# A third buffer for v, a fifth for the exponentials, and stores of x that enter the queue one tile later

## The chip, the core and the metric

The kernel runs on one NeuronCore of a Trainium2 chip. The metric is device time in microseconds (us) of one launch, lower is better. The core has five engines that run side by side, each in its own order and tied to the others by semaphores: TensorE (PE in the rows; PEld is its weight load), VectorE (DVE), ScalarE (ACT), GpSimd (POOL) and SyncE (SP, which here does nothing but issue DMAs). What an engine or a queue has to wait for holds back everything that stands behind it in that engine's order.

## What is computed

Bucketed attention over 4 batches x 8 heads, 768 positions, head dimension 64, and then a mixture of experts on its output.

```python
q_bucket = np.sum(q_bits * powers, axis=-1)          # 6 sign bits of q @ proj; k the same
mask = q_bucket[:, :, :, None] == k_bucket[:, :, None, :]
scores = np.where(mask, scale * np.matmul(q, k.transpose(0, 1, 3, 2)), -1000000000.0)
attn = np.exp(scores - np.max(scores, axis=-1, keepdims=True))
attn = attn / (np.sum(attn, axis=-1, keepdims=True) + 1e-09)
x = np.matmul(attn, v)                                # -> (3072 tokens, 512)
...
e_idx = np.argmax(x @ w_gate + modality_bias[modality_id], axis=1)
out[mask_e] = gate_w[mask_e, None] * (np.maximum(x[mask_e] @ w1[e], 0.0) @ w2[e])
```

## The kernel before

The attention works on 16 pairs of heads, `i` = 0 to 15; pair `i` belongs to batch `i // 4`. While the scores of pair `i` are computed, the operands of pair `i + 2` are prepared and the maxima of pair `i + 1` taken. Each pair has six key tiles `kt`.

- `load(i)` (L110) brings q and k of a pair into `xt`; `load_v(i)` (L116) brings v into `vt`, from a pool of `CFG["v"]` buffers (L100). A new `vt` may be loaded only when TensorE has done the last product with the `vt` that the buffer held, so with two buffers the load for pair `i + 1` waits for the products of pair `i - 1`.
- `turn(i)` (L153) prepares the operands. ScalarE copies `xt` into the rounded `hx` (L166), once for each half x = 0 (q) and x = 1 (k); GpSimd or VectorE subtracts to get the remainder (L168; for the pairs in `RELIEF` both on VectorE); SP issues three SBUF-to-SBUF moves out of `hx` for each half (`move`, L151). `hx` has one buffer: its copy for the next pair waits until all six moves out of it have landed. The moves write into one of three sets of operand tiles, `a_..g` and `b_..g`, and wait until TensorE has finished the scores that used that set.
- `signs(i)` and `patterns(i)` follow, with four more moves out of the b and a tiles.
- `score(i)` (L276) issues score matmuls into two PSUM buffers `pss`; ScalarE takes the exponentials (L285, L292) into a buffer of `pbuf`, `NPB = CFG["npb"]` buffers used in a ring; GpSimd adds each of them to the running sum `sp` (L295). `weigh()` (L306) is the generator that multiplies with v (L319) into `psu`, and ScalarE copies that to `ut` (L324).
- `finish(b)` and `finish_x(b, lo, hi)` (L386) end a batch: per 128-token tile `tt`, four transposes of `ut`, a VectorE multiplication by the reciprocal sums into `xs` (L395, two buffers), and a store of `xs` to `x_d` in DRAM (L397), on SP for batches 0 to 2 and on ScalarE's queue for the last. For batches 0 to 2 the six tiles are spread over two pairs: tiles 0, 1, 2 in the third pair of the next batch and 3, 4, 5 in its fourth (pairs 6 and 7, 10 and 11, 14 and 15).
- `route` scatters a small table entry for each token (L607, six scatters a batch, GpSimd).

The order on TensorE and SP in the attention part is written out by hand: `PLAN` has a string for each `kt`, and each letter advances one generator (S scores, M maxima, T turn of pair `i + 2`, A products with v, L and l the loads, x and y a tile of `finish_x`). ScalarE, VectorE and GpSimd are put in order by the framework's scheduler, from its own model of when inputs are ready. The experts follow (from L713 on), over the SBUF that the attention has given back.

Of the kernel before, what the change touches and what calls it, by code (L numbers as in the profile page):

```python
# [18 lines left out]
B, H, S, D = 4, 8, 768, 64  # L19
# [3 lines left out]
REST = S - MAIN  # L23
NP = B * H // 2
BIG = 2.0 ** 100
CFG = dict(spd=(15,), fxs=3, wy=(0.3, 0.71), hpf=0, he=0, hn=0, hm=0, avp=(1, 2, 3, 4, 5, 6), avs=(2,), early=2, pj=7, w3=(0, 0.9), x3=(0, 1), nmd=1, man=(), man0=2, hpo=0, hpe=0, p0=(0, 1), p1=(0, 0.25), p2=(0, 0.4), p3=(0.4, 0.9), s0=4, rc='DDDD', rq=(1, 2), tq=(3, 3, 1, 1, 0, 0), wh=(0.5, 0.78), ws=(0.78, 1.05), n2=2, psx=2, psm=2, pss=2, npb=4, ut=8, qk=3, v=2, wm=(0, 0.9), wf=(0.04, 1.02), wx=(0.3, 0.71), sub="DPPD", fx='D', fx3='R', raw=4, wp=7, LS=4, LL=7, pn=0, rv=(0,), rs='DDPP', r1=(0, 0.5), r2=(0, 1), avg=1, fub=2, fd=1, pm=(), fj=0, fxe=0.5)
P = 128

LAG = 3
# [53 lines left out]
def attention(ctx, actx, tc, a, x_d, route, setup, early_slots, early_tables, latest, adds, bias):  # L83
    nc = tc.nc
    v = a["v"]
# [3 lines left out]
    spool = ctx.enter_context(tc.tile_pool(name="spool", bufs=2))  # L89
    upool = ctx.enter_context(tc.tile_pool(name="upool", bufs=CFG["ut"]))  # L90
    bp = ctx.enter_context(tc.tile_pool(name="bp", bufs=1))
    bp.tile([P, 48], F32, name="pad2")
    ps_x = ctx.enter_context(tc.tile_pool(name="ps_x", bufs=CFG["psx"], space=PSUM))
    xt = actx.enter_context(tc.tile_pool(name="xt", bufs=2))
    hxp = actx.enter_context(tc.tile_pool(name="hxp", bufs=1))
    gens = []
    for g in range(3):
        opp = actx.enter_context(tc.tile_pool(name=f"opp{g}", bufs=1))
        gens.append({n: [opp.tile([P, 2, S], F32R, name=f"{n}_{h}g{g}") for h in range(2)] for n in ("a", "b")})
    ldv = actx.enter_context(tc.tile_pool(name="ldv", bufs=CFG["v"]))  # L100
    sm = actx.enter_context(tc.tile_pool(name="sm", bufs=4))
    const = actx.enter_context(tc.tile_pool(name="const", bufs=1))
    ps_m = actx.enter_context(tc.tile_pool(name="ps_m", bufs=CFG["psm"], space=PSUM))
    ps_s = actx.enter_context(tc.tile_pool(name="ps_s", bufs=CFG["pss"], space=PSUM))
    flags = actx.enter_context(tc.tile_pool(name="flags", bufs=2))
# [27 lines left out]
    bits = [const.tile([P, HALF], BF16, name=f"bits{j}") for j in range(2)]  # L133
    pbuf = [const.tile([P, 2, S], F32, name=f"pb{j}") for j in range(CFG["npb"])]
    pat32 = pbuf[0][:, 0, 0:512].rearrange("p (a h c) -> p a h c", a=2, h=2)
# [171 lines left out]
    def weigh():  # L307

        for i in range(NPR):
            t = st[i]  # L310
            t["u"] = [ps_u.tile([P, MAIN], F32, name=f"psu{j}") for j in range(2)]
            for part in range(2):
                w = COLS[part].stop - COLS[part].start
                nc.tensor.matmul(t["u"][part][:, 0:w], vsb[i % 2], t["lone"][:, COLS[part]], start=True, stop=False, skip_group_check=True)
            for kt in range(NT):
                for part in range(2):
                    w = COLS[part].stop - COLS[part].start
                    for h in range(2):
                        nc.tensor.matmul(t["u"][part][64 * h:64 * h + 64, 0:w], t["v"][:, h, kt], t["pb"][kt][:, h, COLS[part]], start=False, stop=(kt == NT - 1), skip_group_check=True)  # L319
                if kt == NT - 1:  # L320
                    ut = upool.tile([P, S], F32, name="ut")
                    for part in range(2):
                        w = COLS[part].stop - COLS[part].start
                        nc.scalar.copy(out=ut[:, COLS[part]], in_=t["u"][part][:, 0:w])  # L324
                    t["ut"] = ut
                yield
# [59 lines left out]
    def finish_x(b, lo, hi, pool=bp, n=2, name="xs"):  # L386
        ts_, rin = fin[b]
        xv = x_d[b * S:(b + 1) * S].rearrange("(p t) d -> p t d", t=NT)
        for tt in range(lo, hi):
            xs = pool.tile([P, 512], F32, name=name, bufs=n)  # L390
            xp = ps_x.tile([P, 512], F32, name="psx")
            for c in range(4):
                nc.tensor.transpose(xp[:, c * P:(c + 1) * P], ts_[c]["ut"][:, tt * P:(tt + 1) * P], ident)
            yield
            nc.vector.tensor_tensor(out=xs.rearrange("p (h d) -> p h d", d=D), in0=xp.rearrange("p (h d) -> p h d", d=D),  # L395
                                    in1=rin[:, tt].unsqueeze(2).broadcast_to([P, 8, D]), op=ALU.mult)
            (nc.scalar if b == B - 1 else nc.sync).dma_start(out=xv[:, tt], in_=xs)  # L397
            yield

    def finish_last():  # L400
# [21 lines left out]
    with tc.manual_schedule(engines={mybir.EngineType.PE, mybir.EngineType.SP}):  # L422
# [17 lines left out]
        avs = weigh()  # L440
        fins = xs = ts = iter(())
        for i in range(NPR):
# [6 lines left out]
            for kt in range(NT):  # L449
                for c in (PLAN if i else PLAN0)[kt]:  # L450
# [4 lines left out]
                    elif c == "T":  # L455
                        next(ts, None)
                    elif c == "P":
                        next(last, None)
                    elif c == "A":
                        next(avs)  # L460
                    elif c == "B":
                        if late:
                            late.pop(0)()
                    elif c == "v":
                        vadds(i)
                    elif c == "V":
                        vsums(i)
                    elif c == "Q":
                        if i > 0:
                            sums(i - 1)  # L470
                    elif c == "L":
                        if i + 3 < NPR:
                            load(i + 3)
                    elif c == "l":
                        if 0 < i < NPR - 1:
                            load_v(i + 1)
                    elif c in FIN[i >= NPR - 4][i % 4]:
                        with tc.issue_after(newest[0]):
                            next(fins, None)
                    elif c == "x" and i % 4 == 2 or c == "y" and i % 4 == 3:  # L480
                        if c == "x" and kt == 0 and i > 4:
                            xs = finish_x(i // 4 - 1, 0, NT)
                        next(xs, None)
                        next(xs, None)
        for _ in avs:
            pass
        sums(NPR - 1)
    return finish, finish_x, ps_x, ident


# [518 lines left out]
```

## Time and profile before

| | |
|---|---|
| three runs, us | 799.78, 802.07, 803.81 (median 802.07) |
| profiled execution, us | 803.15, its span 801.4 |
| mean granted TensorE clock | 0.989 |
| busy: PE, PEld, DVE, ACT, POOL, us | 754.0, 522.1, 499.7, 413.5, 438.7 |
| attention part | up to about 490 us, experts from there |

The span runs from the first to the last instruction; the profiled execution's own time lies 1.75 us above it. A busy time is the union of an engine's instructions; weight loads overlap matmuls.

### The profile page before, as it was taken

How to read it: one execution, taken by the hardware profiler on the slowest of the kernel's cores; microseconds unless marked ns; L12 is line 12 of the kernel's file. 1: busy time of each engine (PE TensorE's matmuls, PEld its weight loads, DVE VectorE, ACT ScalarE, POOL GpSimd, SP SyncE). 2: the span in 40 equal slices, each digit the busy share in tenths (PEclk: the TensorE clock that was granted, in tenths of full speed). 3: DMA queues.
4: the chain of work that ended last, by engine and by line, in shares of the span. 5: the costliest groups of instructions: out<-in, count | busy, mean ns of one | idle time of the engine just before them, and what ended most of it. 6: DMA issues, size and time to landing. Idle time of an engine off the chain costs nothing.

```text
span 801.4 us, 11627 instructions
## 1 busy us (share of the span) xinstructions
PE 754.0 (94%) x4060; PEld 522.1 (65%) x4060; DVE 499.7 (62%) x839; ACT 413.5 (52%) x730; POOL 438.7 (55%) x321
## 2 busy tenths in 40 slices
PE   4799999999999899999989999999999999999996
PEld 1555566556565456655555555888888888888885
DVE  6787677578787477787677948764344242752422
ACT  3566676665656466657546456324253334633423
POOL 7298889778869578869847895034120204202002
PEclk9999999999999899999999999999999999999998
DMA  6665534343358333455320275467352435843311
GB/s 204 151 179 158 145 94 136 99 123 107 116 113 155 98 99 107 120 132 159 102 64 25 45 196 201 159 99 229 115 175 81 168 91 178 273 140 124 127 54 60
DMA packets 59573, 104.24 MB, mean 130 GB/s; under 512 B 9709, under 2 KB 30829, under 8 KB 59504
## 3 DMA queue, kind: packets, MB, share of 16 engines
q1 hardware_dynamic: 53424, 88.23, 39.7%
q0 software_dynamic: 4928, 13.14, 5.2%
q10 hardware_dynamic: 1152, 2.03, 0.9%
q8 instruction: 34, 0.56, 0.3%
q14 instruction: 35, 0.29, 0.1%
HBM read 59.89 MB, written 13.33 MB: 91 GB/s over the span
## 4 chain that ended last, share of the span: by engine, by line
PE 65%; DVE 14%; issue 9%; ACT 5%; DMA 4%; POOL 1%; SPq 1%; POOLq 0%; ACTq 0%; DVEq 0%
PE psu L319 12%; PE pss L273 8%; PE pss L274 6%; PE hps L799 4%; PE hps L800 4%; PE hps L801 4%; PE psm L217 4%; PE yps L845 3%; PE yps L843 3%; PE yps L844 3%; PE psm L223 3%; ACT pb L285 2%; DMA x_d<-y 2%; DVE mx L219 2%; PE psx L188 2%
## 5 line engine op out<-in xcount | busy, mean ns | idle before, releaser
L295 POOL TENSOR_TENSOR sp<-sp,pb 128x768 f32<-128x768 f32 x124 | 232.2, 1895 | 18.8 <-ACT pb L292 18.0
L285 ACT ACTIVATE pb<-pss 128x512 f32<-128x512 f32 x192 | 114.1, 598 | 113.8 <-PE pss L274 103.1
L219 DVE TENSOR_REDUCE mx<-psm 128x1 f32<-128x512 f32 x192 | 130.4, 687 | 58.0 <-PE psm L217 57.4
L752 DVE TENSOR_TENSOR w<-raw,w 128x1024 fp32r<-128x1024 f32 x64 | 79.5, 1249 | 96.0 <-ACT w L750 95.4
L319 PE MATMUL psu<-pb,vt 128*64 128x512 f32 (+1 forms) x768 | 134.4, 492 | 0.0
L750 ACT CAST w<-raw 128x1024 fp32r<-128x1024 f32 x64 | 66.9, 1051 | 74.6 <-PE yps L845 65.6
L319 PEld LDWEIGHTS psu<-pb,vt 128*64 128x64 f32 x768 | 50.8, 136 | 69.1 <-issue 58.3
L295 POOL TENSOR_TENSOR sp<-pb,pb 128x768 f32<-128x768 f32 x31 | 58.9, 1920 | 54.1 <-ACT pb L292 54.0
L273 PE MATMUL pss<-a_0g 128*128 128x512 f32 x192 | 80.3, 418 | 7.6 <-ACT pb L285 6.7
L770 POOL DMA_INDIRECT xg<-x_d,tb x18 | 22.8, 1267 | 117.7 <-DMA tb<-tab 112.4
L843 PE MATMUL yps<-w,hl 128*128 128x512 f32 x208 | 82.7, 397 | 0.0
L845 PE MATMUL yps<-w,hh 128*128 128x512 f32 x208 | 81.3, 391 | 0.0
L844 PE MATMUL yps<-w,hh 128*128 128x512 f32 x208 | 81.0, 389 | 0.0
L799 PE MATMUL hps<-xh,w 128*128 128x512 f32 x192 | 75.7, 394 | 0.1
L800 PE MATMUL hps<-xl,w 128*128 128x512 f32 x192 | 74.9, 390 | 0.4 <-DVE xl L789 0.4
L801 PE MATMUL hps<-xh,w 128*128 128x512 f32 x192 | 74.8, 390 | 0.0
L225 DVE TENSOR_REDUCE mx<-psm 128x2 f32<-128x512 f32 x96 | 66.2, 690 | 13.5 <-PE psm L223 11.7
L273 PE MATMUL pss<-a_1g 128*128 128x512 f32 x192 | 69.2, 360 | 3.4 <-ACT pb L292 3.4
L805 ACT ACTIVATE hh<-hps 128x512 fp32r<-128x512 f32 x48 | 28.7, 598 | 73.6 <-PE hps L801 73.6
L274 PE MATMUL pss<-b_0g 128*128 128x512 f32 x192 | 66.1, 344 | 0.0
L274 PE MATMUL pss<-b_1g 128*128 128x512 f32 x192 | 65.7, 342 | 0.0
L806 DVE SCALAR_TENSOR_TENSOR hl<-hps,hh 128x512 fp32r<-128x512 f32 x48 | 33.0, 688 | 50.9 <-ACT hh L805 50.8
(203 smaller groups left out, 1367.4 us busy)
## 6 DMA issues: line engine op xcount, KB each, us to landing
raw<-moe_w SPq DMA_DIRECT2D x64, 512.0 KB, 3.7
xt<-qk SPq DMA_DIRECT2D x31, 384.0 KB, 3.9
vt<-v SPq DMA_DIRECT2D x16, 384.0 KB, 3.9
a_0g<-hx SPq DMA_DIRECT2D x30, 192.0 KB, 3.4
a_1g<-hx SPq DMA_DIRECT2D x30, 192.0 KB, 3.7
x_d<-xs SPq DMA_DIRECT2D x18, 256.0 KB, 2.0
b_1g<-a_1g SPq DMA_DIRECT2D x17, 192.0 KB, 2.9
b_0g<-a_0g SPq DMA_DIRECT2D x17, 192.0 KB, 2.7
```

Source lines behind the costliest of these rows:

```text
L219: newest[:] = [nc.vector.tensor_reduce(out=mx[:, qt + j, 1 - h, 0:1], in_=mp, axis=AX.X, op=ALU.max).ins]
L273: nc.tensor.matmul(out, t["s1"][h][:, ks], t["m1"][h][:, cs], start=True, stop=False)
L274: nc.tensor.matmul(out, t["s2"][h][:, ks], t["m2"][h][:, cs], start=False, stop=True)
L285: nc.scalar.activation(t["pb"][kt][:, h, 0:MAIN], sp, AF.Exp, scale=0.125)
L295: add = (nc.vector if h and i in CFG["spd"] else nc.gpsimd).tensor_tensor(out=t["sp"][:, h], in0=(t["pb"][0] if kt == 1 else t["sp"])[:, h ...
L319: nc.tensor.matmul(t["u"][part][64 * h:64 * h + 64, 0:w], t["v"][:, h, kt], t["pb"][kt][:, h, COLS[part]], start=False, stop=(kt == NT - 1 ...
L799: nc.tensor.matmul(hps, lo[:, c, fs], xh[:, c], start=(c == 0), stop=False)
L800: nc.tensor.matmul(hps, hi[:, c, fs], xl[:, c], start=False, stop=False)
L801: nc.tensor.matmul(hps, hi[:, c, fs], xh[:, c], start=False, stop=(c == 3))
L843: nc.tensor.matmul(yps[g], hl[fc][:, gs], hi[:, fb], start=(fc == 0), stop=False)
L844: nc.tensor.matmul(yps[g], hh[fc][:, gs], lo[:, fb], start=False, stop=False)
L845: nc.tensor.matmul(yps[g], hh[fc][:, gs], hi[:, fb], start=False, stop=(fc == 7))
```

## The change

Two numbers of the table `CFG` are raised: the exponentials get a fifth buffer and v a third. In `finish_x` the store of a tile is no longer issued behind its multiplication: it is kept in the list `done` and issued when the generator is asked for the next tile, ahead of that tile's transposes. The last tile of a batch, and all tiles of the last batch, are stored at once as before.

```diff
 CFG = dict(
...
-    npb=4, ut=8, qk=3, v=2,
+    npb=5, ut=8, qk=3, v=3,
...
+        done = []
         for tt in range(lo, hi):
+            if done:
+                done.pop()()
             xs = pool.tile([P, 512], F32, name=name, bufs=n)
...
             nc.vector.tensor_tensor(out=xs..., in0=xp..., in1=rin..., op=ALU.mult)
-            (nc.scalar if b == B - 1 else nc.sync).dma_start(out=xv[:, tt], in_=xs)
+            done.append(partial((nc.scalar if b == B - 1 else nc.sync).dma_start, out=xv[:, tt], in_=xs))
+            if b == B - 1 or tt == hi - 1:
+                done.pop()()
             yield
```

TensorE and VectorE carry out the same instructions in the same order in both programs. On SP the stores move, on ScalarE some of the `hx` copies, on GpSimd the additions over v (L251 to L253). The names below are tiles; a number behind the last underscore is the tile's buffer or its place in the program. Lines behind the edit are 5 higher in the changed program (a store is L392 when deferred, L402 when issued at once).

SP in pair 7 before, from the moves of half x = 0 for pair 9 to the moves of its signs; `x_d` is the DRAM copy of x, and the three stores are those of tiles 3, 4 and 5 (the number behind `xs` tells them apart):

```order
L151 DMA b_1g2_123<-hx_2380 64x768
L397 DMA x_d_57<-xs_2386 128x512
L397 DMA x_d_57<-xs_2448 128x512
L151 DMA a_0g2_120<-hx_2380 64x768
L151 DMA a_1g2_121<-hx_2380 64x768
L151 DMA b_0g2_122<-hx_2380 64x768
L120 DMA vt_2488<-v 128x2x384
L397 DMA x_d_57<-xs_2490 128x512
L151 DMA b_1g2_123<-b_0g2_122 64x768
```

The same place in the changed program; the numbers of `xs` are one higher for the same tile, so 2252 is tile 2, 2387 tile 3, 2449 tile 4 and 2491 tile 5:

```order
L151 DMA b_1g2_123<-hx_2380 64x768
L392 DMA x_d_57<-xs_2252 128x512
L392 DMA x_d_57<-xs_2387 128x512
L151 DMA a_0g2_120<-hx_2380 64x768
L151 DMA a_1g2_121<-hx_2380 64x768
L151 DMA b_0g2_122<-hx_2380 64x768
L120 DMA vt_2488<-v 128x2x384
L392 DMA x_d_57<-xs_2449 128x512
L402 DMA x_d_57<-xs_2491 128x512
L151 DMA b_1g2_123<-b_0g2_122 64x768
```

The moves of half x = 1 and the load of v stood behind the store of tile 4; they stand behind the store of tile 3 now. At the matching place of pair 6 they stood behind the store of tile 0 and stand behind no store now.

ScalarE in pair 8 before, at the `hx` copies for pair 11 (2973), between the exponentials of key tiles 1 and 2 (`pb1`, `pb2`):

```order
L292 ACTIVATE pb1_161<-pss_2710 128x2x256
L324 COPY ut_2730<-psu0_2537 128x512
L324 COPY ut_2730<-psu1_2538 128x256
L166 CAST hx_2973<-xt_2645 128x768 x2
L285 ACTIVATE pb2_162<-pss_2739 128x512
```

The same place in the changed program, where the ring of five gives these two key tiles the buffers `pb4` and `pb0`:

```order
L292 ACTIVATE pb4_164<-pss_2711 128x2x256
L166 CAST hx_2974<-xt_2646 128x768
L324 COPY ut_2731<-psu0_2538 128x512
L324 COPY ut_2731<-psu1_2539 128x256
L166 CAST hx_2974<-xt_2646 128x768
L285 ACTIVATE pb0_160<-pss_2740 128x512
```

One of the two copies has moved ahead of the copies of `ut`. In pair 7 the copies for pair 10 move further. Behind the copies of `ut` ScalarE runs L285 twice, L292, L285 twice, L292 and `nm` (L235); both copies stood behind that `nm`, and now the first stands behind the first L285 and the second behind the first L292.

## Rows read from the trace of the kernel before

**Rows 1.** The page, busy time of TensorE (share of the span, instructions)

```profile
PE 754.0 (94%) x4060; PEld 522.1 (65%) x4060; DVE 499.7 (62%) x839; ACT 413.5 (52%) x730; POOL 438.7 (55%) x321
```

**Rows 2.** Windows: stretch, length, busy per engine (instructions), clock, DMA share, GB/s

```profile
234.30:270.40 36.10, 31.08 (x162) 17.87 (x166) 21.20 (x35) 19.39 (x37) 29.82 (x22) 0.87 0.75 140
356.50:384.80 28.30, 27.28 (x162) 15.86 (x165) 20.31 (x34) 19.26 (x37) 26.37 (x19) 1.00 0.62 163
```

**Rows 3.** Timeline, TensorE: start, us, instruction [idle before <- what ended it]

```profile
243.34 0.39 PE L273 MATMUL pss<-a_0g 128*128 128x256 f32 x1 [1.82 <-ACT pb L285]
...
265.27 0.58 PE L273 MATMUL pss<-a_0g 128*128 128x256 f32 x1 [3.10 <-ACT pb L285]
```

**Rows 4.** Windows of 4 us behind those two gaps

```profile
244.00:248.00 4.00, 4.00 (x16) 2.77 (x15) 2.06 (x3) 3.68 (x8) 3.82 (x5) 0.57 1.04 123
...
264.00:268.00 4.00, 2.73 (x14) 1.55 (x14) 0.69 (x1) 2.30 (x4) 1.64 (x3) 0.57 0.35 114
268.00:272.00 4.00, 4.00 (x17) 1.40 (x14) 1.63 (x3) 0.60 (x1) 3.77 (x3) 0.57 0.40 98
```

**Rows 5.** Timeline, ScalarE, in pairs 7 and 8

```profile
231.54 1.31 ACT L285 ACTIVATE pb<-pss 128x512 f32<-128x512 f32 x2 [1.46 <-PE pss L274]
...
241.23 1.56 ACT L166 CAST hx<-xt 128x768 fp32r<-128x768 f32 x2 [2.95 <-DMA vt<-v]
...
256.96 0.59 ACT L292 ACTIVATE pb<-pss 128x512 f32<-128x512 f32 x1
259.40 0.86 ACT L324 COPY ut<-psu 128x512 f32<-128x512 f32 x2 [1.85 <-PE psu L319]
263.16 1.56 ACT L166 CAST hx<-xt 128x768 fp32r<-128x768 f32 x2 [2.90 <-DMA vt<-v]
```

**Rows 6.** Timeline, ScalarE, the same copies in pairs 11 and 12

```profile
360.49 1.57 ACT L166 CAST hx<-xt 128x768 fp32r<-128x768 f32 x2
...
379.80 1.57 ACT L166 CAST hx<-xt 128x768 fp32r<-128x768 f32 x2 [0.18 <-ACT ut L324]
```

**Rows 7.** Timeline, SP's issues in pairs 7 and 8

```profile
225.52 6.55 SPq L397 DMA_DIRECT2D x_d<-xs  x2
...
233.32 0.59 SPq L151 DMA_DIRECT2D b_0g<-hx  x1
234.01 0.61 SPq L120 DMA_DIRECT2D vt<-v  x1
...
253.61 0.46 SPq L151 DMA_DIRECT2D b_0g<-hx  x1
259.86 0.39 SPq L120 DMA_DIRECT2D vt<-v  x1
```

**Rows 8.** DMA issues of 232.1 to 234: count, KB each, us to landing

```profile
b_0g<-hx SPq DMA_DIRECT2D x1, 192.0 KB, 7.7
```

**Rows 9.** DMA issues of 247.7 to 254

```profile
b_1g<-hx SPq DMA_DIRECT2D x1, 192.0 KB, 12.9
b_0g<-hx SPq DMA_DIRECT2D x1, 192.0 KB, 9.2
```

**Rows 10.** DMA issues of 366.9 to 371.2

```profile
b_0g<-hx SPq DMA_DIRECT2D x1, 192.0 KB, 4.4
```

**Rows 11.** The page, DMA issues over the whole span, median us to landing

```profile
a_1g<-hx SPq DMA_DIRECT2D x30, 192.0 KB, 3.7
```

**Rows 12.** DMA issues of 232 to 262, then of 354 to 384: the scatters

```profile
tab<-recs,posi POOLq DMA_INDIRECT x6, 7.8
...
tab<-recs,posi POOLq DMA_INDIRECT x6, 5.2
```

**Rows 13.** Waits over the span: us in total, times, longest

```profile
SPq L120 <- PE psu L319: 77.0, 11, 14.6
...
POOL va L251 <- DMA vt<-v: 21.4, 10, 4.3
...
ACT pb L285 <- POOL sp L295: 2.6, 2, 2.3
```

More of the change, by code (lines that the diff above doesn't have):

```diff
@@ L25 @@
 BIG = 2.0 ** 100
-CFG = dict(spd=(15,), fxs=3, wy=(0.3, 0.71), hpf=0, he=0, hn=0, hm=0, avp=(1, 2, 3, 4, 5, 6), avs=(2,), early=2, pj=7, w3=(0, 0.9), x3=(0, 1), nmd=1, man=(), man0=2, hpo=0, hpe=0, p0=(0, 1), p1=(0, 0.25), p2=(0, 0.4), p3=(0.4, 0.9), s0=4, rc='DDDD', rq=(1, 2), tq=(3, 3, 1, 1, 0, 0), wh=(0.5, 0.78), ws=(0.78, 1.05), n2=2, psx=2, psm=2, pss=2, npb=4, ut=8, qk=3, v=2, wm=(0, 0.9), wf=(0.04, 1.02), wx=(0.3, 0.71), sub="DPPD", fx='D', fx3='R', raw=4, wp=7, LS=4, LL=7, pn=0, rv=(0,), rs='DDPP', r1=(0, 0.5), r2=(0, 1), avg=1, fub=2, fd=1, pm=(), fj=0, fxe=0.5)
+CFG = dict(spd=(15,), fxs=3, wy=(0.3, 0.71), hpf=0, he=0, hn=0, hm=0, avp=(1, 2, 3, 4, 5, 6), avs=(2,), early=2, pj=7, w3=(0, 0.9), x3=(0, 1), nmd=1, man=(), man0=2, hpo=0, hpe=0, p0=(0, 1), p1=(0, 0.25), p2=(0, 0.4), p3=(0.4, 0.9), s0=4, rc='DDDD', rq=(1, 2), tq=(3, 3, 1, 1, 0, 0), wh=(0.5, 0.78), ws=(0.78, 1.05), n2=2, psx=2, psm=2, pss=2, npb=5, ut=8, qk=3, v=3, wm=(0, 0.9), wf=(0.04, 1.02), wx=(0.3, 0.71), sub="DPPD", fx='D', fx3='R', raw=4, wp=7, LS=4, LL=7, pn=0, rv=(0,), rs='DDPP', r1=(0, 0.5), r2=(0, 1), avg=1, fub=2, fd=1, pm=(), fj=0, fxe=0.5)
 P = 128
```

## The prediction

> **What bounds the kernel now.** I read the page first, then a table of windows by pair of heads, then the timeline of each engine where two like stretches differ. The reader is to see this. TensorE is busy for 94% of the span, the others for 65% at most [rows 1], so the change can only give what TensorE loses to waits and to a lower clock. Each pair in the attention part takes TensorE some 28 us, from one matmul of the signs to the next. One takes 36.10 us, from 234.3 to 270.4; the pair at the same place of the next batch, 356.5 to 384.8, does the same work with the same letters of the plan and takes 28.30 us, each with 162 records of TensorE [rows 2]. The excess is 36.10 - 28.30 = 7.8 us.
>
> It has two causes, twice each. TensorE stands still for 1.82 us until 243.34 and for 3.10 us until 265.27, both times for an exponential [rows 3]. Behind each stop its clock is granted at a mean of 0.57, between the two levels of 1.2 and 2.4 GHz, in the 4 us from 244 and the 8 us from 264 [rows 4]. Work withheld by the clock is 3 x 0.43 x 4 = 5.2 us, less about 0.6 for the 1.27 us to 265.27 in which TensorE had nothing to run: 4.6. With the idle time, 1.82 + 1.7 = 3.5 us hang on the first stop and 3.10 + 2.9 = 6.0 on the second, 9.5 together. The length of the stretch gives 7.8, since the twin has small gaps of its own; I scale the parts to that: 2.9 and 4.9 us.
>
> What held the exponentials is in ScalarE's order: a copy to hx waited for 2.95 us until 241.23 and another for 2.90 us until 263.16 [rows 5]. The row names the load of v as what ended it, but the copy reads no v: it needs the one buffer of hx free, so all six moves of the pair before landed. Their last was issued at 233.32 and took 7.7 us to land, to 241.0 [rows 7, 8]; in the second case 253.61 + 9.2 = 262.8 [rows 7, 9]. Both fit the copies' starts within 0.4 us. In the twin the same copies begin without such a wait [rows 6].
>
> **The first stop: -2.9 us.** Why was the move as late as 233.32? SP ran into two stores at 225.52 and came out at 232.07 [rows 7]: the second, that of tile 4, waits for VectorE's multiplication, and three moves and the load of v stand behind it. Now the store at that place is tile 3's, which could be issued at 225.52 already, and tile 2's ahead of it waits for nothing new. So the three moves go about 6.5 us earlier, the last at 233.32 - 6.5 = 226.8; at the span's median of 3.7 us [rows 11] it lands at 230.5. ScalarE's first copy has moved up too: it stands behind the first of the two exponentials that begin at 231.54 and take 1.31, so at 232.2 [rows 5]. The margin is 1.7 us and the stop goes. With 7.7 us to land [rows 8] the move lands at 234.5, ScalarE stands for 2.3 us instead of 2.95, and hardly anything is gained: this term lies between -2.9 and -0.3. I take -2.9, because the issue now falls before the stretch of slow landings.
>
> **The second stop: -4.9 us.** The moves for pair 10 wait for TensorE's last scores of pair 7, which come 2.9 us earlier when the first stop goes: the last is issued by 253.61 - 2.9 = 250.7. ScalarE now meets one of the two copies ahead of ut, behind the L292 that ends at 256.96 + 0.59 = 257.55, so at 254.6. If the move takes the twin's 4.4 us [rows 10] it lands at 255.1: half a microsecond late, of which TensorE, with two buffers of scores in front of it, sees nothing. If it takes 9.2 as now [rows 9], it lands at 259.9, ScalarE stands for 5.3 us instead of 2.90, and the stop stays, longer by up to 2.4 us. The term lies between -4.9 and +2.4. Of the two landings 4.4 is nearer to the median of 3.7 [rows 11], and the transfers that were in the queue with these moves, a load of v and three moves, have gone out earlier; I take -4.9.
>
> **The edits that I cost at nothing.** The third buffer of v ends SP's wait for the products, 77.0 us in 11 times, 14.6 at most, and the 21.4 us for which GpSimd waits for v [rows 13]. Behind that load on SP stand four moves whose results TensorE needs for the scores two pairs on, a whole pair (28 us) away; GpSimd follows ScalarE and is busy for 55% [rows 1]. That slack is the cover; were it gone, the longest of the waits, 14.6 us once, would bound the gain, and a load of v that now lands beside moves could cost half a microsecond of landing. The value is 0. The fifth buffer of exponentials ends ScalarE's waits for GpSimd's additions, 2.6 us in two [rows 13]; TensorE's rows name none of them, so -2.6 to 0, value 0. The deferred stores: a tile's multiplication reuses the buffer of two tiles before, whose store now goes out about one tile later. Tile 4's multiplication ends just before 232.07 and needs tile 2's store, issued by 225.52 [rows 7]: over 6 us ahead, value 0, up to the wait of one store if SP is held by moves. The experts keep their instructions and their order on TensorE and VectorE; their buffers lie over those of the attention and shift with them, which I bound by 0.5 us either way, since the additions that read the last exponentials end about where the first hidden layer is written.
>
> **The sum.** 803.15 - 2.9 - 4.9 = 795.35 us for an execution like the profiled one (span 801.4 and 1.75 around it). The median of the runs shown is 802.07, 1.1 lower; I do not know how much of that 1.1 lies in the two stops, so I leave the sum as it is: 795.4.
>
> A rule on the clock gives another sum. The Trainium skill, "TensorE: Matmul & The Clock Gate", section "HAM oscillation", counts a throttled stretch at half of its duration, on top of the idle time that led to it. By that rule the whole 9.5 would be given back and the time would be 793.7; the twin's length says 7.8, and I keep the row.
>
> **Rivals.**
> 1. The second stop stays (27%). Six scatters of the routing table run in each of the two stretches, and their own landings rise and fall with those of the moves: 7.8 us median in the slow one, 5.2 in the twin [rows 12]. The change leaves the scatters alone. If the stretch from 232 to 262 stays slow because of them, only the first term comes: 803.15 - 2.9 = 800.2, and by the median of the runs 799.1. For it: 12.9 and 9.2 us for moves that begin well after the store of tile 4 [rows 9]. Against: the twin has the same six scatters, and its moves take 4.4 [rows 10]. The Trainium skill, "DMA: Bandwidth & Descriptors", section "Specifications", says that transfers below 512 bytes are read, modified and written by the DMA engines; the entries of the table are that small, so the page speaks for this rival, and the difference between the stretches for something besides.
> 2. Slower (11%). ScalarE runs in its written order, and the scheduler has put the hx copies 2 to 6 us further ahead, on its own view of when moves land. The place is pairs 7, 8, 11 and 12; it decides from landings of about 5.4 us on in pairs 7 and 11 (3.7 plus the margin of 1.7). With 7.7 us there and 9.2 in pair 8, ScalarE stands for 2.3, 5.3 and 2.3 us where it now stands for 2.95 and 2.90: 4.0 us more, and one more stretch at the lower clock, 1.7: 803.15 + 5.7 = 808.9.
> 3. No change (15%). The stops are partly this execution's own: the runs spread over 4.0 us, and 799.78 is 3.4 below the profiled execution. If other executions lose little there, or the time comes back as a wait for VectorE behind it, the result is 800 to 803, say 801.5.
>
> **How the numbers follow.** My forecast has 47%, with a range of its own from 792.5 (the sum by the clock's rule, less the 1.1 of the median) to 798. The rivals have 27, 11 and 15%. The range that holds 8 in 10 goes from 791.5, where 2.6 us of the fifth buffer come on top of part of that, to 803.5, which takes in rivals 1 and 3 and leaves out the slower one. Half a percent of 802.07 is 4.0 us, about what a measurement of this kernel can tell from no change: faster is under 798.1, slower over 806.1. Faster holds nearly all of the forecast and a good quarter of rival 1: 54%. Slower is rival 2: 11%. The rest is 35%.
>
> **What would show it.** Right: SP's three moves for half x = 1 of pair 9 issued within a microsecond of the store of tile 3, 6 us ahead of the store of tile 4; no wait in front of the hx copies of pairs 7 and 8; no gap of TensorE over 1 us and no clock under 1 between the signs of pair 9 and of pair 10; that stretch at 28 to 29 us, all others as before. Rival 1 shows a single gap with a lower clock at the copies of `ut` in pair 8. Rival 2 shows waits of ScalarE for DMA in front of hx in pairs 11 and 12, where there are none now. My prediction is wrong if the stretch comes down and the end does not, or if the moves go out early and land as late as before.

## The result

The changed kernel takes 810.31 us (median of 4 runs, 809.66 to 811.06); the kernel before, beside it, 802.83 us (799.78 to 803.81). The ratio is 1.010, interval 1.0074 to 1.0126 (here and below the ratio on record, which is not the quotient of the two medians): the change costs about 7.5 us, where the forecast was a gain of 7.8. The profiled execution of the changed kernel took 810.90 us, with a span of 809.0; the one before took 803.15.

### The profile page after: what moved, and what is told of

Read it like the earlier page. It is cut to its first block, busy times and chain, and to the rows that moved or that the text cites. A ratio compares the mean times of both kernels' runs of the same rounds, so it can differ in the third digit from the quotient of the medians.

```text
span 809.0 us, 11610 instructions
## 1 busy us (share of the span) xinstructions
PE 753.6 (93%) x4060; PEld 522.7 (65%) x4060; DVE 509.0 (63%) x839; ACT 413.3 (51%) x730; POOL 438.4 (54%) x321
## 4 chain that ended last, share of the span: by engine, by line
PE 64%; DVE 13%; issue 10%; ACT 7%; DMA 2%; POOL 2%; SPq 1%; another core or an unknown queue 1%; ACTq 0%; POOLq 0%; DVEq 0%
PE psu L319 11%; PE pss L273 8%; PE pss L274 6%; PE hps L804 4%; PE hps L806 4%; PE hps L805 4%; PE yps L850 4%; PE yps L848 4%; PE psm L217 4%; PE yps L849 4%; ACT pb L285 3%; PE psm L223 2%; DVE b_1g L168 2%; PE psx L188 1%; DVE mx L219 1%
## 5 line engine op out<-in xcount | busy, mean ns | idle before, releaser
L295 POOL TENSOR_TENSOR sp<-sp,pb 128x768 f32<-128x768 f32 x124 | 231.0, 1887 | 46.5 <-ACT pb L292 41.7
L285 ACT ACTIVATE pb<-pss 128x512 f32<-128x512 f32 x192 | 114.1, 598 | 116.2 <-PE pss L274 108.6
L295 POOL TENSOR_TENSOR sp<-pb,pb 128x768 f32<-128x768 f32 x31 | 59.0, 1923 | 40.8 <-ACT pb L292 40.7
L225 DVE TENSOR_REDUCE mx<-psm 128x2 f32<-128x512 f32 x96 | 66.2, 690 | 11.4 <-PE psm L223 9.7
```

The source lines that it names most:

```text
L285: nc.scalar.activation(t["pb"][kt][:, h, 0:MAIN], sp, AF.Exp, scale=0.125)
L295: add = (nc.vector if h and i in CFG["spd"] else nc.gpsimd).tensor_tensor(out=t["sp"][:, h], in0=(t["pb"][0] if kt == 1 else t["sp"])[:, h ...
```

## The profile after

The page, the line that answers [rows 1]:

```profile
PE 753.6 (93%) x4060; PEld 522.7 (65%) x4060; DVE 509.0 (63%) x839; ACT 413.3 (51%) x730; POOL 438.4 (54%) x321
```

No engine has more instructions than before. One has clearly more busy time: VectorE, 509.0 us where it was 499.7. TensorE's is the same, so the span grew by TensorE's waits. The windows of the two stretches of [rows 2], with the same columns, each from the same matmul of the signs to the next:

```profile
234.30:268.90 34.60, 29.35 (x162) 16.82 (x166) 24.13 (x34) 17.98 (x36) 29.31 (x22) 0.90 0.56 123
354.40:388.90 34.50, 29.33 (x163) 17.81 (x166) 24.97 (x34) 17.84 (x35) 27.97 (x21) 0.90 0.57 122
```

The slow stretch has come down only from 36.10 to 34.60, and its twin, 28.30 before, is as slow now. In both VectorE (the third busy time) is busy for 24 to 25 us, against 21.2 and 20.3. Matched record by record (4060 in each), TensorE of the changed kernel stands level with before at 241 us, 3.0 us ahead at 262, 1.7 ahead at 271, 2.0 ahead at 366, 4.1 behind at 386 and 440, and 8.1 behind at 545, from where it stays.

So the first stop is gone. SP's issues, which answer [rows 7]:

```profile
217.82 7.94 SPq L392 DMA_DIRECT2D x_d<-xs  x2
225.86 0.47 SPq L151 DMA_DIRECT2D a_0g<-hx  x1
226.69 0.47 SPq L151 DMA_DIRECT2D a_1g<-hx  x1
227.21 0.59 SPq L151 DMA_DIRECT2D b_0g<-hx  x1
```

The last move of half x = 1 goes out at 227.21, where it was 233.32, and ScalarE's copies to hx in pair 7 wait for nothing, at 231.94 and 233.63 (in [rows 5] the first stood 2.95 us). Then ScalarE in pairs 8 and 12, at the copies of [rows 5, 6]:

```profile
260.97 0.83 ACT L166 CAST hx<-xt 128x768 fp32r<-128x768 f32 x1 [6.44 <-DVE b_1g L168]
...
383.14 0.83 ACT L166 CAST hx<-xt 128x768 fp32r<-128x768 f32 x1 [2.79 <-DVE b_1g L168]
```

It now waits for 6.44 and 2.79 us, and what ends the wait is no transfer: it is VectorE's subtraction L168, which reads the one buffer of hx (at 383.14 one of 1.96 us). TensorE's gaps, which answer [rows 3]:

```profile
263.84 0.58 PE L273 MATMUL pss<-a_0g 128*128 128x256 f32 x1 [4.70 <-ACT pb L285]
...
372.21 0.49 PE L242 MATMUL psx<-identr,nm 128*128 128x128 f32 x2 [3.71 <-ACT nm L235]
...
386.01 0.39 PE L273 MATMUL pss<-a_0g 128*128 128x256 f32 x1 [1.07 <-ACT pb L285]
```

The gap of 3.10 us has become 4.70, and two are new. The clock falls behind the first two, as in [rows 4]; the windows there:

```profile
262.00:266.00 4.00, 2.16 (x10) 1.55 (x14) 1.03 (x2) 2.87 (x6) 0.17 (x1) 0.50 0.66 148
...
374.00:378.00 4.00, 4.00 (x14) 3.42 (x13) 2.33 (x4) 2.45 (x6) 1.65 (x2) 0.50 0.22 53
```

The granted clock there is 0.50, the lower of the two levels. What VectorE does in front of these gaps, timeline of VectorE:

```profile
255.28 5.61 DVE L168 TENSOR_TENSOR b_1g<-xt,hx 128x768 fp32r<-128x768 f32 x1
...
365.24 4.95 DVE L168 TENSOR_TENSOR b_0g<-xt,hx 128x768 fp32r<-128x768 f32 x1
370.11 0.68 DVE L225 TENSOR_REDUCE mx<-psm 128x2 f32<-128x512 f32 x1
```

These are the subtractions L168 of `turn`, which read `hx`. The same instruction on tiles of the same shape takes 0.95 us at 245.12, and 5.61 and 4.95 us here. At 255.28 it holds back the copy to hx and the exponentials behind that; at 365.24 it holds back the maxima of L225, and with them nm, for which TensorE waits. GpSimd beside it:

```profile
254.50 0.98 POOL L612 DMA_INDIRECT tab<-recs,posi  x1 [0.17 <-issue]
255.51 3.61 POOL L295 TENSOR_TENSOR sp<-pb,pb 128x768 f32<-128x768 f32 x2
259.07 0.99 POOL L251 TENSOR_TENSOR va<-vt 128x384 f32<-128x384 f32 x1
...
364.80 0.96 POOL L612 DMA_INDIRECT tab<-recs,posi  x1 [0.30 <-issue]
365.79 3.57 POOL L295 TENSOR_TENSOR sp<-sp,pb 128x768 f32<-128x768 f32 x2
369.53 1.52 POOL L612 DMA_INDIRECT tab<-recs,posi  x1 [0.17 <-issue]
```

Both subtractions begin while a scatter (L612) runs, 0.78 and 0.44 us into it, and end 0.83 us after GpSimd's additions behind it: 259.07 + 0.99 = 260.06 and 260.89, 365.79 + 3.57 = 369.36 and 370.19. The same two places before, GpSimd and then VectorE:

```profile
257.64 4.32 POOL L295 TENSOR_TENSOR sp<-pb,pb 128x768 f32<-128x768 f32 x2 [0.69 <-ACT pb L292]
...
365.84 0.96 POOL L607 DMA_INDIRECT tab<-recs,posi  x1 [0.30 <-issue]
366.82 1.02 POOL L251 TENSOR_TENSOR va<-vt 128x384 f32<-128x384 f32 x1
367.92 1.06 POOL L252 TENSOR_TENSOR va<-va 128x128 f32<-128x128 f32 x1
```

```profile
258.30 1.96 DVE L168 TENSOR_TENSOR b_1g<-xt,hx 128x768 fp32r<-128x768 f32 x1
...
367.29 1.38 DVE L168 TENSOR_TENSOR b_0g<-xt,hx 128x768 fp32r<-128x768 f32 x1
```

In pair 11 the additions over v (L251 to L253) stood behind the fourth scatter. In the changed program they stand behind the first and second, the third and fourth scatters come 1.2 us later in pair 7 and, against TensorE, 1.0 us later in pair 11, and the subtraction meets the long additions L295 instead. In pair 8 GpSimd paused for 0.69 us between the sixth scatter and the additions.

A subtraction that begins in a scatter need not be long. The one of 0.95 us in the changed kernel, and the scatter that it begins in, 0.28 us after its start:

```profile
245.12 0.95 DVE L168 TENSOR_TENSOR b_0g<-xt,hx 128x768 fp32r<-128x768 f32 x1
...
244.84 0.96 POOL L612 DMA_INDIRECT tab<-recs,posi  x1 [0.30 <-issue]
```

Over all traces twelve subtractions out of hx begin in a scatter with GpSimd's work right behind it: the four that begin 0.12 to 0.28 us into it take 0.95 us, the eight that begin 0.43 us or more into it take 4.67 to 5.95.

## The experiments

Three theories were put to the test. A: the loss is VectorE's subtraction behind GpSimd's additions, and it is the third buffer of v that moves GpSimd against VectorE. B: the hx copies, moved ahead in ScalarE's order, do the harm (rival 2 of the prediction). C: a subtraction that begins in a scatter stands behind the additions that follow on GpSimd. Later C was sharpened: additions that follow on a scatter without a break run as a train, and VectorE gets in only where a GpSimd instruction must wait for the one before it. A hand-over is the place where one GpSimd instruction ends and the next begins.

**The parts of the change.** Each is the kernel before with one edit or two.

```diff
 e1_stores_only: the edit of finish_x alone
 e2_v3_only:     -v=2  +v=3
 e3_npb5_only:   -npb=4  +npb=5
 e4_stores_v3:   finish_x and v=3
```

> Stores deferred, v at 2 buffers and the exponentials at 4, as before. On SP, TensorE, VectorE and ScalarE the order is that of the changed kernel; on GpSimd the additions over v move in pairs 7 and 11 only. Theory A (the loss is VectorE's subtraction L168 standing behind GpSimd's additions, and GpSimd's phase comes from the third buffer of v): the first stop goes, the subtractions in pairs 8 and 12 stay near 2 us, the time is 797 to 801. Theory B (the hx copies that were moved ahead on ScalarE cost it, whatever GpSimd does): 806 to 811, with gaps of TensorE over 3 us near 264 and 372 as in the changed kernel.

> Third buffer for v alone. ScalarE, VectorE and TensorE keep the order of the kernel before; GpSimd takes its additions over v earlier in most pairs. Theory A: GpSimd's shifted phase makes one or more of the subtractions L168 of pairs 10 and 14 (in before 1.2 to 2.0 us) take 4 us or more, and the time is 804 to 809. Theory B: the copies stand where they stood, the time is 801 to 804 and both stops of pairs 7 and 8 are there.

> Fifth buffer of exponentials alone; no engine's order changes. Both theories: 801 to 804, no difference from before beyond its spread.

> The change without the fifth buffer of exponentials; every engine's order is that of the changed kernel. Theories A and B: 808 to 812, as the changed kernel. If it is at 803 or below, the fifth buffer is what lets GpSimd come into the way, and both theories miss a part.

| | us | ratio to before (median 801.29), interval | long subtractions, us |
|---|---|---|---|
| stores | 807.30 | 1.0065 (1.0042 to 1.0087) | 4.67 at 255.84, 4.93 at 365.35 |
| v | 801.88 | 0.9995 (0.9972 to 1.0019) | 4.88 at 257.04 |
| exponentials | 801.33 | 0.9995 (0.9972 to 1.0018) | none |
| stores and v | 809.08 | 1.0081 (1.0051 to 1.0110) | 5.62 at 255.29, 4.96 at 365.21 |

The third buffer of v as the cause falls: the deferred stores alone carry most of the loss. With 807.30 us and gaps of TensorE of 3.71 us before 263.41 and 3.69 before 372.31 they came out as theory B expected; only the later runs tell B from C. With v alone one subtraction is long, as theory A expected, and the time is not: TensorE's gap behind it is 3.21 us, about the 3.10 that stood there before. What v adds to the stores (809.08 against 807.30) lies within the intervals, as does what the fifth buffer adds. Every long subtraction began in a scatter with additions right behind it; this is where theory C came from. The first two runs also take the first stop away or shorten it (no gap with stores alone, 1.10 us with v alone).

The profiled execution with the fifth buffer alone (800.53 us) shows something else. ScalarE, VectorE, TensorE and SP have the order of the kernel before, and yet the copies of pair 8 wait for nothing and the second stop is missing:

```profile
262.30 1.57 ACT L166 CAST hx<-xt 128x768 fp32r<-128x768 f32 x2
```

TensorE is 3.6 us ahead by 271 there, while the median, 801.33, is that of the kernel before. So the second stop need not be in every execution.

**The scatters left out.** Both kernels, without the twelve scatters of batches 0 to 2.

```diff
-        for t in range(NT):
+        for t in range(NT if b == B - 1 else 0):
```

> The changed kernel without the scatters of the routing table for batches 0 to 2 (12 of them beside pairs 7, 8, 11 and 12; left out, so the experts gather dummy rows for those tokens). Theory C (a subtraction L168 that begins while GpSimd is in a scatter stands behind all additions that follow without a break): no subtraction takes over 3 us, no gap of TensorE over 1.5 us near 264, 372 and 386, the time is 793 to 798. Theory B (hx copies ahead of ut wait for moves that land late, or for anything else): the gaps stay, 803 to 810.

> The kernel before without the same scatters, as the measure for the run without them of the changed kernel. If the scatters slow the landings of the moves, both stops of pairs 7 and 8 shrink: 795 to 799. If they do not, 800 to 802. Theory C: the changed kernel without scatters is no slower than this one.

The changed kernel takes 799.35 us (0.9970, 0.9946 to 0.9993), 1.4 above what theory C expected; the one before 797.63 (0.9947, 0.9929 to 0.9965), so the changed one is 1.7 us the slower, where theory C expected it to be no slower; the intervals overlap. No subtraction is longer than 2.5 us in either, and at 386 us both stand 6.8 to 7.4 us ahead of the kernel before: without scatters neither has the two stops, so in these traces the stops of before hang on the scatters as well as the new ones (the edit also moves what follows them on GpSimd). The moves out of hx land faster without them: the two b_0g moves of 225 to 262 us take 4.3 us (median), where they took 8.4. The copies to hx are ahead in ScalarE's order in the first of the two and cost little up to there (two gaps of TensorE of 1.04 and 1.05 us that the second run does not have), which speaks against theory B. Its profiled execution (804.93 us, the slowest of its runs) loses 6.6 us near 495; ScalarE waits there for a load of the experts' weights, 3.65 us until 494.75, and TensorE for 4.17 us behind it.

**The additions over v put back.** The changed kernel, with L251 to L253 of pairs 8 and 12 held behind the fourth scatter, as they stood before.

```diff
+        with tc.issue_after(SCATTERED[-3]) if i in (8, 12) else nullcontext():
             nc.gpsimd.tensor_tensor(out=a1, in0=v[:, :, 0:3], ...)
```

> The changed kernel with the additions over v for pairs 8 and 12 put back behind the fourth scatter on GpSimd, where they stood before; SP, ScalarE, VectorE and TensorE as in the changed kernel. Theory C: the subtraction near 365 begins beside the additions over v instead of in a scatter and takes under 2 us; the one near 255 still begins in the sixth scatter and takes over 4: 804 to 807, with the gap near 264 and none near 372. Theory B: no difference from the changed kernel, 809 to 811.

796.96 us, ratio 0.9938 (0.9915 to 0.9962): better than theory C expected, and faster than both kernels, with every copy to hx where the change had put it. That settles B: where the subtractions are short, the copies ahead cost nothing that is seen. No subtraction takes over 2.6 us. The one near 255 us was expected to stay long; it began at 255.75, ahead of the sixth scatter at 256.14, so there it is the moment that changed. GpSimd at the place of pair 11:

```profile
357.66 0.96 POOL L617 DMA_INDIRECT tab<-recs,posi  x1 [0.30 <-issue]
358.64 1.02 POOL L255 TENSOR_TENSOR va<-vt 128x384 f32<-128x384 f32 x1
359.74 1.06 POOL L256 TENSOR_TENSOR va<-va 128x128 f32<-128x128 f32 x1
```

**A second scatter put forward.** The same, with the sixth scatter directly behind the fifth.

```diff
+            if t < NT - 1 and latest:
+                behind = latest[0]
-            with tc.issue_after(latest[0]) if b < B - 1 else nullcontext():
+            with tc.issue_after(behind) if b < B - 1 else nullcontext():
```

> As the run before, and the sixth scatter of a batch put directly behind the fifth, ahead of the additions between them; nothing is left out. Theory C: no subtraction of pairs 10 and 14 begins in a scatter, all take under 3 us, both gaps go, the time is 795 to 800. Theory B: 809 to 811.

811.41 us, ratio 1.0117 (1.0091 to 1.0144): a miss. No subtraction begins in a scatter, and yet two are the longest of all. VectorE and GpSimd there:

```profile
256.54 6.76 DVE L171 TENSOR_TENSOR b_1g<-xt,hx 128x768 fp32r<-128x768 f32 x1
```

```profile
253.38 0.97 POOL L619 DMA_INDIRECT tab<-recs,posi  x1 [0.31 <-issue]
254.37 3.59 POOL L299 TENSOR_TENSOR sp<-sp,pb 128x768 f32<-128x768 f32 x2
257.93 3.60 POOL L299 TENSOR_TENSOR sp<-pb,pb 128x768 f32<-128x768 f32 x2
261.50 0.98 POOL L255 TENSOR_TENSOR va<-vt 128x384 f32<-128x384 f32 x1
262.56 1.06 POOL L256 TENSOR_TENSOR va<-va 128x128 f32<-128x128 f32 x1
```

The subtraction begins in the second of four additions, passes three hand-overs of GpSimd without getting in, and ends 0.82 us after L255, which L256 has to wait for. So to begin in a scatter is not the condition; to meet a train behind a scatter is what all the long ones share. The same was then counted over all traces, the later runs too: subtractions out of hx met 152 hand-overs from one addition L295 to the next without a break in trains that do not begin at a scatter, and got in at each; in trains that do, they met 12 and got in at none.

**A gap in the train, and its control.** The changed kernel with a copy of one column of the sum onto itself in each step of the pairs of the scatters: between the two additions, where the second then stands behind an instruction that waits for the first; and, as the control, behind both.

```diff
 e9_gap:  +  gap = nc.gpsimd.tensor_copy(out=t["sp"][:, 0, 0:1], in_=t["sp"][:, 0, 0:1]).ins   # h == 0
          +  with tc.issue_after(gap) if h and ... else nullcontext():                          # h == 1
 e10_tail: + nc.gpsimd.tensor_copy(out=t["sp"][:, 1, 0:1], in_=t["sp"][:, 1, 0:1])              # behind both
```

> The changed kernel with one small GpSimd copy (one column of the running sum onto itself) put between the two additions of a step in the pairs of the scatters, so that the second addition stands behind an instruction that waits for the first; the order on all other engines is the changed kernel's. Theory C, sharpened (additions that follow directly on a scatter run as a train and let VectorE's subtraction in only where a GpSimd instruction has to wait for the one before it): the subtractions that took 5.61 us at 255.28 and 4.95 us at 365.24 take at most an addition and their own 0.83 us after it, 2 to 3.1 us; the gaps of 4.70 us before 263.84 and 3.71 us before 372.21 fall under 2 us, and the time is 799 to 805 us. Rival (the scatter itself, its descriptors or its traffic, holds VectorE, and a gap between the additions changes nothing): the subtractions stay over 4.5 us and the time is 809 to 813 us.

> Control for the run with the gap: the same small copies in the changed kernel, one for each step, but where they wait for nothing, behind the step's two additions (the schedule puts most of them directly behind a scatter); no other engine's order changes. Sharpened theory C: the trains stay, the subtractions near 255 and 365 us stay over 4 us, and the time is 808 to 812 us. If a mere shift of GpSimd by ten small instructions decides (the phase alone), one or both of the long subtractions may go, and the time is 797 to 806 us.

With the gap 796.70 us, 0.9932 (0.9908 to 0.9956), below the range expected; the control 803.82 us, 1.0032 (1.0005 to 1.0059), a miss for sharpened theory C, which expected 808 to 812, and inside the range of a mere shift of GpSimd. The first does not prove the gap: its subtractions at the two places took 0.95 and 1.36 us because they no longer met the trains at all. In the control one long subtraction is gone by its moment alone (it began 0.12 us into a scatter, at 360.04, and took 0.95 us), and one is left. VectorE and GpSimd there:

```profile
370.22 5.95 DVE L168 TENSOR_TENSOR b_1g<-xt,hx 128x768 fp32r<-128x768 f32 x1
```

```profile
369.64 1.00 POOL L614 DMA_INDIRECT tab<-recs,posi  x1 [0.17 <-issue]
370.65 0.19 POOL L300 COPY sp<-sp 128x1 f32<-128x1 f32 x1
370.80 3.61 POOL L295 TENSOR_TENSOR sp<-pb,pb 128x768 f32<-128x768 f32 x2
374.37 0.98 POOL L251 TENSOR_TENSOR va<-vt 128x384 f32<-128x384 f32 x1
375.31 0.91 POOL L300 COPY sp<-sp 128x1 f32<-128x1 f32 x1
```

A gap of TensorE of 5.05 us before 379.13 follows it. The copy of 0.19 us directly behind the scatter, which waits for nothing there, did not break that train. VectorE got in behind L251, and the instruction that then had to stand is the other small copy, 0.91 us long at 375.31. It begins before L251 ends (375.31 against 374.37 + 0.98 = 375.35), so it did not wait for L251. VectorE thus also got in where GpSimd had no wait, and the "only" of sharpened theory C does not hold.

**The stores alone, with the additions over v put back.** Two buffers for v and four for the exponentials, as before.

> The stores deferred, with two buffers for v and four for the exponentials as before, and GpSimd's additions over v in pairs 7 and 11 held behind the fourth scatter, as they stand in the kernel before. If the gain of the run with the additions over v put back (796.96 us) comes from the stores alone and the two buffers are worth nothing: 796 to 799 us, no subtraction over 3 us. If the fifth buffer of exponentials or the third of v carry part of it: 799 to 803 us. If the order on GpSimd does not matter without them: 807 us, as with the stores alone.

795.58 us, ratio 0.9922 (0.9894 to 0.9951): the first of the three outcomes, 0.4 us below its range. What the two buffers add to that lies within the intervals. Windows of the two stretches:

```profile
234.30:262.90 28.60, 27.73 (x161) 16.25 (x161) 21.02 (x35) 18.55 (x36) 26.07 (x18) 1.00 0.57 133
350.00:379.00 29.00, 28.14 (x165) 16.63 (x164) 20.95 (x35) 18.02 (x35) 27.17 (x20) 1.00 0.57 136
```

Both are about the twin's 28.30 [rows 2], at the full clock.

**A gap where the train is surely met.** The kernel of 811.41 us with two GpSimd instructions more in the whole program: the small copy, once in each of its two trains of four additions, between the second and the third. No other engine's order changes, and nothing ahead of the long subtractions moves.

```diff
+                    with tc.issue_after(GAP[0]) if kt == 1 and i in (8, 12) else nullcontext():
...
+                if kt == NT - 1 and i in (7, 11):
+                    GAP[:] = [nc.gpsimd.tensor_copy(out=t["sp"][:, 1, 0:1], in_=t["sp"][:, 1, 0:1]).ins]
```

> The kernel with the sixth scatter directly behind the fifth (811.41 us), with two more GpSimd instructions in the whole program: a copy of one column of the running sum onto itself, behind the last addition of pairs 7 and 11 and ahead of the next pair's first. It waits for the addition before it, and stands in the middle of the train of four additions; nothing ahead of the long subtraction's start is moved. Sharpened theory C (the train behind a scatter lets VectorE in only where a GpSimd instruction waits for the one before it): the subtractions of 6.76 us at 256.54 and 6.79 us at 377.51 become 2.0 to 2.4 us (1.43 us to the end of the addition they meet, 0.83 us of their own), the gaps of 5.80 and 5.78 us go, and the time is 795 to 800 us. Rival (the two scatters hold VectorE for their own time, gap or no gap): 6 to 7 us again, and 810 to 813 us. A third way, in which VectorE gets in only when the additions end: 5.9 us, as 0.98 us of the additions over v fall away at most, and 809 to 811 us.

800.18 us, 0.9966 (0.9948 to 0.9985), 11.2 us under the kernel without the two copies; the profiled execution took 797.95. VectorE and GpSimd:

```profile
256.17 2.28 DVE L171 TENSOR_TENSOR b_1g<-xt,hx 128x768 fp32r<-128x768 f32 x1
...
371.06 2.31 DVE L171 TENSOR_TENSOR b_1g<-xt,hx 128x768 fp32r<-128x768 f32 x1
```

```profile
254.00 3.62 POOL L300 TENSOR_TENSOR sp<-sp,pb 128x768 f32<-128x768 f32 x2
257.68 0.81 POOL L305 COPY sp<-sp 128x1 f32<-128x1 f32 x1
258.46 3.62 POOL L300 TENSOR_TENSOR sp<-pb,pb 128x768 f32<-128x768 f32 x2
```

6.76 and 6.79 us have become 2.28 and 2.31, as expected: VectorE gets in at the end of the addition at 257.62 and holds the copy for its own 0.83 us. Rival and third way are out. The median is 0.2 us above the range expected. The copy waits 0.06 us for the addition before it; whether it is that wait or the small copy as such that lets VectorE in, this run does not tell, as no copy without a wait was put at the same place.

## Why the prediction was wrong

- **The first stop, -2.9 us: right.** 3.0 us are gained by 262 us in the changed kernel, by the moves at 227.21. The worry about the landings (7.7 us) did not come true: the copies waited for nothing.
- **The second stop, -4.9 us: right in size, and hidden by something else.** In the stores alone with the additions put back TensorE gains 2.7 us from 241 to 262 and 5.5 more by 271, 8.2 together where the sum had 7.8. In the changed kernel the stop stays with 4.70 us for a new reason. Both bounds given for the term came from landings; the wait that took its place is for VectorE.
- **The step that failed: "the edits that I cost at nothing", the deferred stores.** I followed their cost in the queue of SP and in the buffer of xs, and gave 0. What the section on the change had shown, that the additions over v move on GpSimd, never entered the sum; I took GpSimd for slack at 55% and VectorE's instructions for constant. The move puts two subtractions of VectorE into trains of additions behind a scatter, at 3.6 us more each (4.95 against 1.38 in pair 11, 5.61 against 1.96 at the start of pair 8), with a stop of TensorE for each and the clock at 0.50 behind it. From 366 to 386 us alone that costs 2.0 + 4.1 = 6.1 us.
- **The other edits.** Third buffer and fifth buffer: 0, as forecast (801.88 and 801.33 against 801.29). For v the zero is partly luck: in its profiled execution TensorE gains 2.9 us from 241 to 271 and loses 2.0 from 440 to 545. The waits of [rows 13] went as expected: GpSimd's for v is 3.7 us in 5 times where it was 21.4 in 10, and nothing came of it.
- **The rivals.** Rival 2 had the time (808.9) and the places, pairs 8, 11 and 12, but not the mechanism: the copies ahead are harmless where the subtractions are short, and no landing decides; the time was met by luck. Rival 1 had the scatters as what slows the stretch, and they are, through the landings and through VectorE too. Rival 3 has something to it: the second stop is missing in one execution with the order of before on ScalarE, VectorE, TensorE and SP. The forecast's own sum, 795.4 us, is what the stores give when GpSimd's order is left as it was: 795.58. That they meet to 0.2 us is luck, since the sum starts from one execution of 803.15 and the profiled execution of this run took 796.98.
- **The end of the attention part.** From 440 to 545 us the changed kernel loses 4.0 us more than before, more than half of its net loss, in gaps of 2.34 us before 453.96 (0.92 before), 1.38 before 497.33 and 1.31 before 538.86. The first is a meeting with GpSimd too. A small VectorE instruction ahead of it, then and now:

```profile
445.80 0.22 DVE L653 SCALAR_TENSOR_TENSOR selx<-kslot,selw 128x16 f32<-128x16 f32 x1
...
449.87 1.67 DVE L658 SCALAR_TENSOR_TENSOR selx<-kslot,selw 128x16 f32<-128x16 f32 x1
```

  At 449.87 it begins 0.20 us into an addition L295 and ends 0.03 us behind it; no scatter is near. In all 14 traces the gap is the duration of this instruction plus 0.7 us (0.92 with 0.22, 1.59 with 0.89, 2.34 with 1.67), so it has 1.4 of the 4.0 us. The runs of 796.96 and 796.70 us, with three buffers for v, have it too, at 2.3 us; the one of 795.58 us, with two, 1.59. What makes the other two gaps stays open.

The Trainium skill, "SBUF — State Buffer", section "SBUF: two separate sides", says that a VectorE instruction with two SBUF inputs and a GpSimd instruction that reads SBUF lock each other out, and that the one that starts first has the shared pair of ports for the whole instruction while the other stands. The 152 hand-overs agree: VectorE stands for the rest of one addition (1.96 us at 258.30 before, 0.66 us into an addition of 1.80). The 12 behind a scatter do not: there it stands for two to four instructions.

## What to carry to other kernels

When a change moves instructions on an engine that looks idle, look at which other engine's instructions grow longer beside it: the price can appear as a longer duration of another engine's instruction, far from the edit, and the waits name only that instruction, not what holds it. Compare the durations of the same instruction over the trace before costing an order at nothing. Where VectorE must get between GpSimd's instructions, a small instruction that waits for its predecessor can be put into GpSimd's row (one copy made 2.28 us of 6.76 here), or long runs of additions can be kept from standing right behind a scatter.

## What was not expected of the hardware

Additions on GpSimd that follow a scatter without a break let VectorE's subtractions in at none of 12 hand-overs; elsewhere they got in at all of 152. One copy of 128 x 1 that waits for the addition before it opened such a train (6.76 us became 2.28). A copy that waits for nothing did not directly behind the scatter, and one did behind L251 (both in the subtraction of 5.95 us), so the wait is not shown to be the condition. A pause of 0.69 us for ScalarE between the scatter and the additions was enough too (before, at 257.64, and a subtraction of 1.96 us). Why a scatter makes the difference no run shows.
